# The last token tile's second layer in two column parts

## The chip, the cores and the metric

The kernel runs on one core of a Trainium2 chip. The metric is the device time of one execution in microseconds; the median of several runs is given. Beside it stands one profiled execution, whose trace lists every instruction with its engine, start and length. TensorE (PE) does the matrix products, VectorE (DVE) and ScalarE (ACT) work on tiles, GpSimd (POOL) does some copies, and SyncE (SP) issues every load and store as a DMA.

## The reference

```python
# q, k, v, alpha: (4, 8, 768, 48) float32
for t in range(S):
    state = alpha[:, :, t, :, None] * state + np.einsum('bhd,bhe->bhde', k[:, :, t], v[:, :, t])
    y[:, :, t] = np.einsum('bhd,bhde->bhe', q[:, :, t], state)
x = y.transpose(0, 2, 1, 3).reshape(3072, 384)
h = x @ w_in                  # (384, 2048)
r = np.maximum(h, 0.0)
out = (r * r) @ w_out         # (2048, 384) -> (3072, 384) float32
```

A gated linear attention over 768 steps feeds a two-layer network with a squared ReLU.

## The kernel before

The 3072 tokens are 24 tiles of 128. The attention is computed in chunks of 128 steps, 24 in all, and each chunk gives one token tile of `x`, transposed, in `xT_big`. The network runs on groups of token tiles: `GN = [4, 1, 1, 2, 2, 2, 2, 2, 2, 2, 2, 2]` (line 537), so the last group, number 11, holds tiles 22 and 23, and the one before it tiles 20 and 21.

The first layer (`add_moe1`, line 553) multiplies `w_in` with `xT_big` into a PSUM bank of 512 columns; ScalarE applies the ReLU and VectorE squares the result into `gT`. The second layer (`add_moe2`, line 592) handles one token tile: sixteen matmuls of 384 columns, one for each slice of the 2048 hidden values, add up in one PSUM bank. Each takes a 128 x 128 block of `gT` as its weights and a slice of `w_out_b` as the moving operand. One copy (`e_ev`, line 612) brings the bank into an SBUF tile `ob`, and one DMA from SP's queue (`e_out`, line 621) stores it, 128 rows of 1536 bytes.

No instruction is issued as the functions are called. Each adds an `Op` to a plan, with a duration, dependencies and a priority. `Plan.run` (line 96) takes the ops greedily in planned time: it gives each a start and an end, chooses the engine where several are allowed (ScalarE or VectorE for the copy, whichever ends first with its latency from `LAT`, line 34), and the PSUM bank, the one that is free earliest of the pool named (`takes`; for the last two groups `M2_LAST`, all five banks). Stores are planned on an engine called OUT, loads on one called DMA; both are issued on SP. A store is planned when its copy is done, and its start is then put off by `late`:

```python
            op.start = t + getattr(op, "late", 0.0)
```

For every store `late` is `OUT_LATE`, 3.5 us (line 623). At the end of `Plan.run` the whole list is sorted by start,

```python
        self.order.sort(key=lambda o: o.start)
```

and line 706 emits the instructions in this order. `pin` (line 234) keeps each engine's instructions in the order in which they are emitted, and SP's too: SP works through its queue in order, and an instruction that waits for its data holds up those behind it.

Of the kernel before, what the change touches and what calls it, by code (L numbers as in the profile page):

```python
# [8 lines left out]
FP32 = mybir.dt.float32  # L9
# [45 lines left out]
def after(op, x=0.0):  # L55
    return (op, x)
# [83 lines left out]
def kernel(  # L140
# [10 lines left out]
    nc = tc.nc  # L151
    B, H, S, D = q.shape
    HD = H * D
    P = 128
# [3 lines left out]
    d_model, d_ff = moe_w_in.shape  # L158
    n_tok = out.shape[0]
    KT = d_model // P  # L160
    FT = d_ff // P
# [6 lines left out]
    out_r = out.rearrange("(tt p) n -> tt p n", p=P)  # L168
# [7 lines left out]
    opool = ctx.enter_context(tc.tile_pool(name="opool", bufs=6))  # L176
# [15 lines left out]
        out=utri_f, in_=utri_f, compare_op=ALU.is_ge, fill=0.0,  # L192
# [10 lines left out]
    for c in range(JN):  # L203
        blk = slice(JP * c, JP * c + JP)
        nc.gpsimd.affine_select(
            out=tri4[blk, 0:JW], in_=tri4[blk, 0:JW], compare_op=ALU.is_ge, fill=0.0,
# [11 lines left out]
    w_out_b = consts.tile([P, FT, d_model], BF16)  # L218
# [15 lines left out]
    def pin(ins):  # L234
        tc.keep_in_program_order(ins)

    def mm(*a, **kw):
        pin(nc.tensor.matmul(*a, **kw))  # L238
# [4 lines left out]
    plan = Plan()  # L243
# [6 lines left out]
    M2_BANKS = sl_bank[4:1:-1]  # L250

    def psum(op, shape, dt):
        i = op.slot.bank
        return banks[i].tile(shape, dt, name=f"bank{i}")
# [6 lines left out]
    def add(eng, dur, emit, *deps, **kw):  # L261
        return plan.add(Op(eng, dur, emit, deps, **kw))
# [38 lines left out]
    def w_dep(which, f):  # L301
        return w_ready[which][[hi > f for hi in W_CUT[which][1:]].index(True)]
# [234 lines left out]
    GN = [4, 1, 1, 2, 2, 2, 2, 2, 2, 2, 2, 2]  # L537
    assert sum(GN) == NT
    GT = [sum(GN[:i]) for i in range(len(GN))]
    NG = len(GN)  # L540
    gT = {}
    NQ = 4
    NGT = 3
    FIRST = sl_bank[4:0:-1]
    M2_LAST = sl_bank[::-1]
    OUT_LATE = 3.5
    RELU_PRIO = -20.0
    RELU_PRIO0 = 0.0
    DUMMY = 1
    sq = {}  # L550
    prog = {"m1": 0.0, "m2": 0.0}

    def add_moe1(g, f0, before, lo=0, hi=None, per=1):
        hi = GN[g] if hi is None else hi
        t0, n = (GT[g] + lo) * P, (hi - lo) * P
        w = per * n
        box = {}
        op = before
        for i in range(per):
            def e_mm(i=i, f=f0 + i):  # L560
                if i == 0:
                    box["ph"] = psum(box["first"], [P, 512], FP32)
                for j in range(KT):
                    mm(box["ph"][:, i * n:(i + 1) * n], lhsT=w_in_b[:, j, f * P:(f + 1) * P],
                       rhs=xT_big[:, j, t0:t0 + n], start=(j == 0), stop=(j == KT - 1))
            deps = [C[s]["x"] for s in range(GT[g] + lo, GT[g] + hi)] + [w_dep("i", f0 + i)]
            deps += [after(op)] if op else []
            takes = M1_BANKS if i == 0 else None
            op = plan.add(Op("PE", 3 * n / 2400.0 + 0.01, e_mm, deps, takes=takes, prio=0.0, lat=0.10 if w < 512 else 0.17))
            op.moe = (1, (hi - lo) * 2.56 / FT)  # L570
            op.opens, op.closes = i == 0, i == per - 1
            if i == 0:
                box["first"] = op

        def e_relu():
            box["r"] = rpool.tile([P, 512], BF16, name="r")
            pin(nc.scalar.activation(box["r"][:, 0:w], box["ph"][:, 0:w], AF.Relu))  # L577
        rl = add("ACT", 0.055 + w / 1190.0, e_relu, op, prio=RELU_PRIO if g > 1 else RELU_PRIO0)
        box["first"].gives = rl

        def e_sq():
            if g not in gT:
                gT[g] = big.tile([P, FT, P * max(GN[g % NGT::NGT])], BF16, name=f"gT{g % NGT}", tag=f"gT{g % NGT}")
            r = box["r"][:, 0:w].rearrange("p (a n) -> p a n", a=per)
            pin(nc.vector.tensor_mul(gT[g][:, f0:f0 + per, lo * P:lo * P + n], r, r))  # L585
        fr = sq[(g - NGT, "free")] if g >= NGT else None
        o = add("DVE", 0.06 + w / 1850.0, e_sq, rl, fr, prio=SQ_PRIO)
        for i in range(per):
            sq.setdefault((g, f0 + i), []).append(o)
        return op  # L590

    def add_moe2(g, tt, before, box, quarters, pools):

        for qd in quarters:
            def e_mm(qd=qd):
                if qd == 0:
                    box["po"] = psum(box["first"], [P, 512], FP32)[:, 0:d_model]
                for kf in range(qd * FT // NQ, (qd + 1) * FT // NQ):
                    mm(box["po"], lhsT=gT[g][:, kf, tt * P:(tt + 1) * P], rhs=w_out_b[:, kf, :],
                       start=(kf == 0), stop=(kf == FT - 1))  # L600
            fs = range(qd * FT // NQ, (qd + 1) * FT // NQ) if g == 0 else range(FT)
            deps = [o for f in fs for o in sq[(g, f)]] + [w_dep("o", fs[-1] if g == 0 else FT - 1)] + ([after(before)] if before else [])
            op = plan.add(Op("PE", 0.65, e_mm, deps, takes=pools if qd == 0 else None, prio=0.1))
            op.moe = (2, 2.56 / NQ)
            if qd == 0:
                box["first"] = op
            op.lat = 0.05
            before = op
        if quarters[-1] < NQ - 1:
            return op  # L610

        def e_ev():
            box["ob"] = opool.tile([P, d_model], FP32, name="ob")
            if ev.eng == "DVE":
                pin(nc.vector.tensor_copy(box["ob"], box["po"]))
            else:
                pin(nc.scalar.copy(box["ob"], box["po"]))  # L617
        ev = add({"DVE": 0.47, "ACT": 0.38}, 0, e_ev, op, prio=-15.0)
        box["first"].gives = ev

        def e_out():
            pin(nc.sync.dma_start(out=out_r[GT[g] + tt], in_=box["ob"]))
        add("OUT", 0.55, e_out, ev, at=0.0).late = OUT_LATE
        return op
# [22 lines left out]
    for g in range(NG):  # L647
        if g == 0:
            last1 = []
            for f in range(0, FT, 4):  # L650
                for parts in FIRST_SETS:
                    for lo, hi in parts[min(f // 4, len(parts) - 1)]:
                        last1.append(add_moe1(g, f, None, lo, hi, per=4 // (hi - lo)))
                        for x in range(f + 4 // (hi - lo), f + 4, 4 // (hi - lo)):
                            last1.append(add_moe1(g, x, None, lo, hi, per=4 // (hi - lo)))
            b1 = last1[-1]
        per = 1 if g == 0 else 4 // GN[g]
        for f in range(FT if g == 0 else 0, FT, per):
            b1 = add_moe1(g, f, b1, per=per)
        if g == 0:  # L660
            boxes = [dict() for _ in range(GN[0])]
            for part in FIRST_PARTS:
                for tt in range(GN[0]):
                    b2 = add_moe2(0, tt, b2, boxes[tt], part, FIRST)
        else:
            for tt in range(GN[g]):
                b2 = add_moe2(g, tt, b2, {}, range(NQ), M2_LAST if g >= NG - 2 else M2_BANKS)
        sq[(g, "free")] = b2

    LEAD = 3.5  # L670
# [64 lines left out]
```

## Time and profile before

| | us |
|---|---|
| median of 3 runs (192.62 to 192.91) | 192.75 |
| the profiled execution | 191.59 |
| its span, first to last instruction | 189.9 |
| PE busy | 181.7 (96%) |
| DVE busy | 127.5 (67%) |
| ACT busy | 123.6 (65%) |
| second-layer matmuls, 384 of them: busy, mean of one | 71.6, 0.326 |
| copies of `ob` on ACT, 23 of 24: mean of one | 0.478 |
| stores, 24 of 192 KB: median from issue to landing | 2.7 |

A matmul's length in the trace is longer than its distance from the next, because matmuls are pipelined: to find what one more costs, the time of a run of equal ones is divided by their number. The granted clock of TensorE is 1.0 throughout. A DMA's line on SP gives the time that SP takes to issue it; the transfer comes later and is seen in the packets and in the landing.

The trace's order of loads and stores on SP ends with the last load at 122.04 us; after that SP issues nothing but stores.

### The profile page before, as it was taken

The page shows a single profiled execution, that of the slowest core. Times are in us where ns is not written, and L with a number is a line of the kernel's source. Part 1 is how long each engine was busy: PE and PEld are TensorE (multiplying, and loading weights), DVE is VectorE, ACT ScalarE, POOL GpSimd, SP SyncE. Part 2 cuts the span into 40 slices and gives each one's busy share as a digit, 9 for nine tenths or more (in the row PEclk, how much of TensorE's full clock was granted, in tenths as well). Part 3 has the DMA queues.
Part 4 walks back from the last instruction along what each step waited for, and adds up shares of the span by engine and source line. Part 5 has one row for each costly group of instructions (what it writes and reads, how often), then busy time and mean ns, then how long its engine had stood idle before and what let it go on. Part 6 is the DMA issues. An engine that isn't in the chain of part 4 may idle for free.

```text
span 189.9 us, 5238 instructions
## 1 busy us (share of the span) xinstructions
PE 181.7 (96%) x2092; PEld 137.6 (72%) x2092; DVE 127.5 (67%) x277; ACT 123.6 (65%) x285; POOL 17.5 (9%) x43
## 2 busy tenths in 40 slices
PE   7898999589999999999999999999999999999993
PEld 2577899357886788868868868868868768768661
DVE  1388889554798999858768768767857857734200
ACT  4667789155897778956955955946956746718321
POOL 8130100101111111121010010010010000000000
PEclk9999999999999999999999999999999999999999
DMA  6999996989999898999999899550110110111012
GB/s 181 226 242 264 299 342 133 350 227 196 246 234 223 183 219 188 213 175 226 202 209 232 174 239 214 108 149 0 43 45 0 47 41 5 41 41 45 12 71 83
DMA packets 104728, 30.22 MB, mean 159 GB/s; under 512 B 96256, under 2 KB 103936, under 8 KB 104704
## 3 DMA queue, kind: packets, MB, share of 16 engines
q1 hardware_dynamic: 104704, 29.89, 67.2%
q8 instruction: 16, 0.26, 0.6%
q14 instruction: 8, 0.07, 0.1%
HBM read 25.17 MB, written 4.72 MB: 157 GB/s over the span
## 4 chain that ended last, share of the span: by engine, by line
PE 84%; DMA 9%; ACT 2%; DVE 2%; issue 1%
PE bank L238 71%; DMA wo<-in_moe_w_out_dram 9%; PE bank L241 8%; PE sc L238 4%; PE st L238 2%; ACT w_out_b L294 1%; DVE w_out_b L292 1%; DVE qkT L371 0%; ACT qkT L369 0%; DVE st L492 0%; ACT A L408 0%; ACT ob L617 0%; DVE w_in_b L292 0%; DVE gT L585 0%; ACT Ainv L412 0%
## 5 line engine op out<-in xcount | busy, mean ns | idle before, releaser
L238 PE MATMUL bank<-xT_big,w_in_b 128*128 128x256 bf16 (+1 forms) x720 | 76.8, 251 | 0.0
L238 PE MATMUL bank<-w_out_b,gT 128*128 128x384 bf16 x384 | 71.6, 326 | 2.1 <-DVE w_out_b L292 2.1
L577 ACT ACTIVATE r<-bank 128x512 bf16<-128x512 f32 x96 | 56.5, 604 | 16.9 <-PE bank L238 14.9
L238 PEld LDWEIGHTS <-w_in_b 128*128 128x128 bf16 x720 | 55.4, 98 | 5.0
L238 PEld LDWEIGHTS <-gT 128*128 128x128 bf16 x400 | 35.6, 97 | 21.0 <-issue 2.1
L585 DVE TENSOR_TENSOR gT<-r 128x512 bf16<-128x512 bf16 x96 | 38.6, 428 | 14.2 <-ACT r L577 13.9
L472 DVE TENSOR_TENSOR sm<-sc,utri_b 128x512 bf16<-128x512 f32 x48 | 30.8, 683 | 3.2 <-PE sc L238 3.0
L617 ACT COPY ob<-bank 128x384 f32<-128x384 f32 x23 | 11.0, 478 | 23.7 <-PE bank L238 23.7
L431 DVE TENSOR_TENSOR qA_s<-qt,A 128x384 bf16<-128x384 f32 x24 | 13.7, 572 | 17.4 <-ACT A L408 17.4
L388 POOL CAST vb<-vt 128x384 bf16<-128x384 f32 x24 | 12.9, 538 | 122.1 <-DMA vt<-in_v_dram 64.0
L371 DVE COPY qkT<-bank 128x1024 bf16<-128x1024 bf16 (+1 forms) x23 | 15.0, 655 | 6.8 <-PE bank L241 6.8
L238 PEld LDWEIGHTS <-qkT 64*128 64x128 bf16 (+1 forms) x272 | 10.9, 95 | 6.7 <-issue 1.9
L408 ACT ACTIVATE A<-bank 128x384 bf16<-128x384 f32 x24 | 12.0, 498 | 4.9 <-PE bank L238 4.7
L497 ACT CAST sb<-st 128x384 bf16<-128x384 f32 x20 | 9.6, 478 | 7.9 <-DVE st L492 7.6
L434 DVE TENSOR_TENSOR kI_s<-kt,Ainv 128x384 bf16<-128x384 f32 x24 | 13.8, 576 | 0.0
L369 ACT CAST xn<-bank 128x384 bf16<-128x384 f32 x24 | 11.6, 483 | 1.5 <-PE bank L238 1.5
L379 ACT ACTIVATE L_s<-at 128x384 bf16<-128x384 f32 x20 | 10.5, 524 | 2.8 <-DMA at<-in_alpha_dram 2.6
L412 ACT ACTIVATE Ainv<-bank 128x384 bf16<-128x384 f32 x24 | 12.0, 502 | 0.0
L238 PE MATMUL bank<-warm 128*128 128x256 bf16 (+1 forms) x48 | 10.0, 345 | 1.3 <-DVE warm L186 1.2
L492 DVE TENSOR_TENSOR st<-st,ae_s 128x384 f32<-128x384 f32 x20 | 11.1, 556 | 0.0
L371 DVE COPY xT_big<-bank 128x384 bf16<-128x384 bf16 x23 | 8.1, 350 | 2.6 <-PE bank L241 2.5
L241 PE MATMUL bank<-ident_bf,kI_s 128*128 128x128 bf16 x96 | 9.3, 219 | 0.5 <-ACT qkT L369 0.5
(52 smaller groups left out, 138.0 us busy)
## 6 DMA issues: line engine op xcount, KB each, us to landing
qt<-in_q_dram SPq DMA_DIRECT2D x24, 192.0 KB, 3.8
kt<-in_k_dram SPq DMA_DIRECT2D x24, 192.0 KB, 3.8
vt<-in_v_dram SPq DMA_DIRECT2D x24, 192.0 KB, 3.9
out_dram<-ob SPq DMA_DIRECT2D x24, 192.0 KB, 2.7
at<-in_alpha_dram SPq DMA_DIRECT2D x20, 192.0 KB, 3.9
wo<-in_moe_w_out_dram SPq DMA_DIRECT2D x4, 768.0 KB, 9.0
wi<-in_moe_w_in_dram SPq DMA_DIRECT2D x4, 384.0 KB, 5.0
wi<-in_moe_w_in_dram SPq DMA_DIRECT2D x2, 768.0 KB, 8.3
```

Source lines behind the costliest of these rows:

```text
L238: pin(nc.tensor.matmul(*a, **kw))
L241: pin(nc.tensor.transpose(*a))
L369: pin(nc.scalar.copy(out_t, in_t))
L371: pin(nc.vector.tensor_copy(out_t, in_t))
L388: pin(nc.gpsimd.tensor_copy(d["vb"], d["vt"]))
L408: pin(nc.scalar.activation(d["A"], d["pm"][:, 0:HD].rearrange("p (h d) -> p h d", h=H), AF.Exp))
L412: pin(nc.scalar.activation(d["Ai"], d["pm"][:, 0:HD].rearrange("p (h d) -> p h d", h=H), AF.Exp, scale=-1.0))
L431: pin(nc.vector.tensor_mul(qA[:, :, 0:D], d["qt"], d["A"]))
L434: pin(nc.vector.tensor_mul(kI[:, :, 0:D], d["kt"], d["Ai"]))
L472: pin(nc.vector.tensor_mul(d["sm"][:, hh], d["sc"][:, hh], utri_b.to_broadcast([P, NP, P])))
L577: pin(nc.scalar.activation(box["r"][:, 0:w], box["ph"][:, 0:w], AF.Relu))
L585: pin(nc.vector.tensor_mul(gT[g][:, f0:f0 + per, lo * P:lo * P + n], r, r))
```

## The change

For the last tile of the last group (tile 23), `add_moe2_last` takes the place of `add_moe2`. It makes two parts, columns 0 to 256 and 256 to 384. Each part has its own PSUM bank, sixteen matmuls, a copy into its columns of one common `ob` tile, and a store of these columns. The first part's store has `late = OUT_LATE`, the second part's `late = 0.0`. All other tiles are as before.

```diff
+    LAST_CUT = 256
...
+    def add_moe2_last(g, tt, before, pools):
+        ob = {}
+        for lo, hi in ((0, LAST_CUT), (LAST_CUT, d_model)):
+            before = add_moe2_cols(g, tt, before, pools, ob, lo, hi)
+        return before
+
+    def add_moe2_cols(g, tt, before, pools, ob, lo, hi):
+        box = {}
+        w = hi - lo
+
+        def e_mm():
+            box["po"] = psum(op, [P, 512], FP32)[:, 0:w]
+            for kf in range(FT):
+                mm(box["po"], lhsT=gT[g][:, kf, tt * P:(tt + 1) * P], rhs=w_out_b[:, kf, lo:hi],
+                   start=(kf == 0), stop=(kf == FT - 1))
+        deps = [o for f in range(FT) for o in sq[(g, f)]] + [w_dep("o", FT - 1), after(before)]
+        op = plan.add(Op("PE", FT * w / 2400.0 + 0.04, e_mm, deps, takes=pools, prio=0.1, lat=0.05))
+        op.moe = (2, 2.56 * w / d_model)
+
+        def e_ev():
+            if lo == 0:
+                ob["t"] = opool.tile([P, d_model], FP32, name="ob")
+            if ev.eng == "DVE":
+                pin(nc.vector.tensor_copy(ob["t"][:, lo:hi], box["po"]))
+            else:
+                pin(nc.scalar.copy(ob["t"][:, lo:hi], box["po"]))
+        ev = op.gives = add({"DVE": 0.06 + w / 940.0, "ACT": 0.05 + w / 1190.0}, 0, e_ev, op, prio=-15.0)
+
+        def e_out():
+            pin(nc.sync.dma_start(out=out_r[GT[g] + tt][:, lo:hi], in_=ob["t"][:, lo:hi]))
+        add("OUT", 0.55 * w / d_model, e_out, ev, at=0.0).late = OUT_LATE if lo == 0 else 0.0
+        return op
...
             for tt in range(GN[g]):
-                b2 = add_moe2(g, tt, b2, {}, range(NQ), M2_LAST if g >= NG - 2 else M2_BANKS)
+                if g == NG - 1 and tt == GN[g] - 1:
+                    b2 = add_moe2_last(g, tt, b2, M2_LAST)
+                else:
+                    b2 = add_moe2(g, tt, b2, {}, range(NQ), M2_LAST if g >= NG - 2 else M2_BANKS)
```

## The prediction

> **What bounds the kernel now.** I read the page's chain first, then its end in order of time, then the timeline of the last 15 us, then the SP queue and the last store's packets.
>
> ```profile
> PE 84%; DMA 9%; ACT 2%; DVE 2%; issue 1%
> ```
>
> TensorE is the path almost throughout, but the change touches only the last token tile (tile 23), so only the end counts. The chain's last pieces (start, length, what):
>
> ```profile
> 169.86 16.79 PE bank L238 x119
> 186.65 0.02 issue
> 186.68 0.48 ACT ob L617
> ```
>
> The timeline of the end (start, length, engine, line, operation; in brackets the idle time before and what ended it):
>
> ```profile
> 176.07 10.56 PE L238 MATMUL bank<-w_out_b,gT 128*128 128x384 bf16 x64
> ...
> 179.38 8.13 SPq L622 DMA_DIRECT2D out_dram<-ob  x4
> 181.47 0.48 ACT L617 COPY ob<-bank 128x384 f32<-128x384 f32 x1 [2.12 <-PE bank L238]
> 184.07 0.48 ACT L617 COPY ob<-bank 128x384 f32<-128x384 f32 x1 [2.12 <-PE bank L238]
> 186.68 0.48 ACT L617 COPY ob<-bank 128x384 f32<-128x384 f32 x1 [2.12 <-PE bank L238]
> ```
>
> The last 64 matmuls are the second layer of tiles 20 to 23, back to back. Each tile is copied out 0.05 us after its last matmul, and its store leaves just after. Tile 22's copy ends at 184.55, so its store is long gone when tile 23's copy ends at 187.16. The last store alone, in the SP queue and in its transfers (40 slices of 187 to 190 us, 0.0725 us each):
>
> ```profile
> 187.18 0.33 SPq L622 DMA_DIRECT2D out_dram<-ob  x1
> ```
>
> ```profile
> DMA  0000000000000379999952000000000000000000
> GB/s 0 0 0 0 0 0 0 0 0 0 0 0 0 143 287 369 430 389 348 389 205 62 0 0 0 0 0 0 0 0 0 0 0 0 0 0 0 0 0 0
> ...
> out_dram<-ob SPq DMA_DIRECT2D x1, 192.0 KB, 1.8
> ```
>
> Issue at 187.18; packets from slice 13 to slice 21, that is from 187.98 to about 188.65 (0.80 us after issue, for 0.67 us); landing 1.8 us after issue, 188.98, so 0.33 us follow the packets. The span ends at 189.9, 0.92 us after the landing. The end is therefore: last matmul, copy 0.48, store 1.80, closing 0.92.
>
> **The steps. 1: matmuls.** Sixteen of 384 columns become sixteen of 256 and sixteen of 128. Pitches: (10.56 - 0.33) / 63 = 0.1624 us at 384 columns; for the others
>
> ```profile
> 170.84 5.40 PE L238 MATMUL bank<-xT_big,w_in_b 128*128 128x256 bf16 x48
> ```
>
> ```profile
> 46.55 1.33 PE L238 MATMUL bank<-xT_big,w_in_b 128*128 128x128 bf16 x21
> ```
>
> give (5.40 - 0.27) / 47 = 0.1091 and (1.33 - 0.22) / 20 = 0.0555 (0.27 and 0.22 are the mean lengths of single ones). Tile 23 starts at 176.07 + 48 x 0.1624 = 183.87. Part 1 hands over at 183.87 + 16 x 0.1091 = 185.61; part 2's last matmul starts 15 x 0.0555 later and ends 0.22 after that, at 186.66 instead of 186.63: +0.03 us. The sixteen added weight loads cost nothing: the 21 matmuls of the second row also had one load each, 98 ns by its row, and still came 55.5 ns apart. Were they not covered, 15 x (0.098 - 0.0555) = 0.64 us would come on top; the row excludes it, so that is no part of the range. The Trainium skill, "TensorE: Matmul & The Clock Gate", section "Back-to-back issue gap", gives some 81 ns for a stream of load and matmul pairs at 128 columns, and this speaks against the change: by it this term would be about 0.4 us larger. The row of 55.5 ns decides.
>
> **2: copies.** Part 1's copy (256 columns) lies under part 2's 0.84 us of matmuls, on a ScalarE that is otherwise idle; uncovered it would delay part 2's copy by its own length, below 0.48. Part 2's copy (128 columns) is in no row. Neighbours:
>
> ```profile
> L577 ACT ACTIVATE r<-bank 128x512 bf16<-128x512 f32 x48 | 28.5, 604 | 12.3 <-PE bank L238 10.9
> L617 ACT COPY ob<-bank 128x384 f32<-128x384 f32 x15 | 7.2, 478 | 19.8 <-PE bank L238 19.8
> ...
> L418 ACT ACTIVATE ae_s<-bank 64x4 f32<-64x4 f32 x9 | 1.5, 169 | 0.2
> ```
>
> Bounds are 0.17 and 0.48; the slopes between these rows (0.81 and 0.98 ns a column) put 128 columns at 0.27 and 0.23. I take 0.25. So the last copy runs from 186.71 to 186.96, 0.20 us earlier than now. If that were all, the end would come earlier.
>
> **3: stores, and the queue they pass.** Here the change moves more than it says. The instruction list is sorted by planned start, and a store's planned start is the planned end of its copy plus `late`: 3.5 for every tile, and for part 1; 0.0 for part 2. A tile's matmuls are planned at 2.6 us. Counting from the planned end of tile 22's matmuls: tile 22's store stands at 0.05 + 0.38 + 0.14 + 3.5 = 4.07; part 2's store at about 1.75 + 0.89 + 0.05 + 0.16 + 0.14 = 2.99; part 1's at 1.75 + 0.05 + 0.27 + 0.14 + 3.5 = 5.70; tile 21's at 4.07 - 2.6 = 1.47. The SP order becomes tile 21, part 2, tile 22, part 1. That SP keeps the list's order shows in mid kernel:
>
> ```profile
> 90.45 0.70 SPq L354 DMA_DIRECT2D at<-in_alpha_dram  x1
> 91.24 0.86 SPq L354 DMA_DIRECT2D qt<-in_q_dram  x1
> 92.19 2.05 SPq L622 DMA_DIRECT2D out_dram<-ob  x1
> ```
>
> That store's copy had ended at 90.12, and two loads still went ahead of it for two microseconds, as the 3.5 asks. So part 2's store, which waits for the very last copy, stands in front of tile 22's store (ready at 184.55) and part 1's (ready at about 186.2: 185.77 + 0.05 + 0.37). Nobody waits for these but the end of the kernel, which now waits for all three: 64 + 192 + 128 KB from 186.98 on, in place of 192 KB from 187.18.
>
> **4: what that queue costs.** SP's gap from the end of one issue to the next is about 0.09 us in that queue (91.24 + 0.86 to 92.19), and an issue into an empty queue 0.33, so the pitch is 0.42. Issues: part 2 at 186.98, tile 22 at 187.40, part 1 at 187.82. Packets of tile 22's store begin at 187.40 + 0.80 = 188.20. Part 1's could begin at 188.62, but share the same sixteen engines; at the rate of the present store (192 KB in 0.67) both are done at 188.20 + 0.67 x 320 / 192 = 189.32. With 0.33 the landing is 189.65, against 188.98: +0.67. Part 2's 64 KB (0.22 us of packets from 187.78) are through before and cost nothing but SP's 0.42; that pitch is the cover. The Trainium skill, "DMA: Bandwidth & Descriptors", section "Rules for kernel authors", advises to coalesce transfers, because small ones are mostly overhead; a sum by it would charge the 64 KB store its whole fixed time, which no row of this trace singles out.
>
> **Sum.** +0.03 (PE) - 0.23 (shorter copy) + 0.84 (two more issues) - 0.22 (64 KB less in the last store) + 0.25 (part 1's packets behind tile 22's) = +0.67, the same. Against the profiled execution of 191.59 (span 189.9 and 1.69 around it) that is 192.26; the median of the runs, 192.75, stands 1.16 above that execution, and carrying this over gives 193.4.
>
> Bounds. Low: a copy of 0.17 and no queueing of packets, 0.67 - 0.08 - 0.25 = +0.34. High: issues that take as long as the stores in mid kernel that found loads in flight (median of all 24 is 0.48, this row's neighbours 0.70 to 0.97): at 0.97 + 0.09 each, part 1 leaves at 189.10 and lands 0.80 + 0.45 + 0.33 later, 190.68: +1.70. I take 0.33, since the four last stores, with no loads about, all show it.
>
> **Rivals.**
> (a) The order of stores stays that of readiness. Then tile 22's and part 1's stores are gone (the latter issued at 186.2) and part 2's lands at 186.98 + 0.80 + 0.22 + 0.33 = 188.33: -0.65, a time of 192.1. This one is faster. It decides at one point: whether SP reaches tile 22's store before it meets part 2's wait. For it: the last four stores now leave 0.02 us after their own copies. Against it: the row at 92.19, and the arithmetic of 2.99 before 4.07.
> (b) The order is turned round as forecast and SP also waits for room in the queue: issues of 0.74, as the store at 86.00 us took, so a pitch of 0.83. Part 1 leaves at 188.64 and lands at 190.22: +1.24, 194.0. For it: all stores with company in the queue took 0.6 or more. Against: their company was loads of small packets.
> (c) The order is turned round, but the queue is cheap: the low bound, +0.34, 193.1, or less, within what can be told. For it: 0.20 us are gained first.
>
> **How the numbers follow.** My forecast 0.72, (a) 0.08, (b) 0.12, (c) 0.08. About 0.2% (0.39 us) can be told from no change. My forecast and (b) lie beyond it, except for a hundredth of mine: slower 0.83. (c) and that hundredth: same 0.09. (a): faster 0.08. The range leaves (a) out, takes in (c) from its end, (b), and the spread of the runs (0.15 each way): 193.0 to 194.1.
>
> **What would show it.** In the profile of the changed kernel: the stores of tiles 20 and 21 at 179.4 and 182.0, then a gap on SP until about 187, then three issues close together; no store between 182.0 and 186.9; transfers of 64, 192 and 128 KB in one block from 187.8 to 189.3; a copy of some 0.25 us ending near 186.96; sixteen matmuls of 128 columns 55 ns apart. A store issued near 184.58 would prove me wrong (rival a); issues of 0.7 us would be (b).

## The result and the profile after

The change makes the kernel slower: a median of 192.95 us against 192.16 over 22 runs each, ratio 1.0047 (95% interval 1.0024 to 1.0069), that is +0.9 us (0.5 to 1.3). The ratio is that of the means, without the one run of the kernel before that lay more than 1.5% above its fastest. The profiled execution has a span of 191.2 us.

The end in the timeline of the changed kernel (start, length, engine, line, operation; L618 and L622 are the two parts, L651 and L656 the other tiles):

```profile
184.62 0.48 ACT L651 COPY ob<-bank 128x384 f32<-128x384 f32 x1 [2.12 <-PE bank L238]
186.37 0.37 ACT L618 COPY ob<-bank 128x256 f32<-128x256 f32 x1 [1.27 <-PE bank L238]
187.26 0.27 ACT L618 COPY ob<-bank 128x128 f32<-128x128 f32 x1 [0.52 <-PE bank L238]
187.55 0.33 SPq L622 DMA_DIRECT2D out_dram<-ob  x1
187.94 0.42 SPq L656 DMA_DIRECT2D out_dram<-ob  x1
188.41 0.42 SPq L622 DMA_DIRECT2D out_dram<-ob  x1
```

Tile 22's copy ends at 185.10, part 1's at 186.74, part 2's at 187.53. All three stores leave after that, part 2's first. What SP waited for says the same: its one wait on a part's copy lasts 4.6 us, with tile 22's store ready behind it for 2.5 us.

```profile
SPq L622 <- ACT ob L618: 4.6, 1, 4.6
```

The transfers of the changed kernel, from 187.0 to 191.2 us in 40 slices of 0.105 us, and the time from issue to landing:

```profile
DMA  0000000000000495028998999960000000000000
...
out_dram<-ob SPq DMA_DIRECT2D x1, 192.0 KB, 2.0
out_dram<-ob SPq DMA_DIRECT2D x1, 128.0 KB, 1.9
out_dram<-ob SPq DMA_DIRECT2D x1, 64.0 KB, 1.5
```

First 64 KB alone, a gap, then 320 KB in one block to 189.9: tile 22's store and part 1's share the engines. The matmuls of the two parts by shape (count, busy us, mean ns):

```profile
L238 PE MATMUL bank<-w_out_b,gT 128*128 128x256 bf16 x16 | 1.9, 272 | 0.0
L238 PE MATMUL bank<-w_out_b,gT 128*128 128x128 bf16 x16 | 1.1, 219 | 0.0
```

For 128 columns, (1.1 - 0.22) / 15 = 0.06 us each; the starts in the trace lie 0.056 apart.

**How the runs were compared.** The profiled span grew by 1.3 us, more than the runs did. Tile 22's copy ends 0.55 us later than before, though the program up to there is the same. In this profile the granted clock was 0.97 over the first 60 us, where it was 1.00 before. In the eleven profiles of this study, taken on several chips, that moment lies anywhere from 182.75 to 185.25 us. Much of the difference between profiles thus arises ahead of the change, and what it is stays open. So each profile is read from the end of tile 22's copy: to the last landing, and from there to the last instruction (the closing). These repeat within 0.02 us. SP's recorded instructions include its waits.

| run | landing | closing | sum | against before | ratio of the times, 95% | SP instructions |
|---|---|---|---|---|---|---|
| before | 4.48 | 0.85 | 5.33 | | | 210 |
| the change | 5.17 | 0.98 | 6.15 | +0.82 | 1.0047 (1.0024 to 1.0069) | 210 |
| e1_ready_order | 4.00 | 1.38 | 5.38 | +0.05 | 1.0010 (0.9980 to 1.0039) | 211 |
| e2_swap_only | 5.01 | 1.02 | 6.04 | +0.71 | 1.0039 (1.0016 to 1.0062) | 209 |
| e3_tile22_first | 4.63 | 0.98 | 5.61 | +0.29 | 1.0009 (0.9983 to 1.0035) | 210 |
| e4_one_store | 4.31 | 0.85 | 5.16 | -0.17 | 0.9978 (0.9949 to 1.0006) | 210 |
| e8_both_late | 3.98 | 1.39 | 5.37 | +0.04 | 1.0007 (0.9976 to 1.0039) | 212 |
| e11_split_tile20 | 4.49 | 1.39 | 5.87 | +0.55 | 1.0056 (1.0022 to 1.0089) | 211 |
| e10_tile20_on_act | 3.98 | 0.98 | 4.97 | -0.36 | 0.9962 (0.9924 to 1.0000) | 210 |
| e12_change_again | 5.17 | 0.98 | 6.15 | +0.82 | 1.0023 (0.9989 to 1.0058) | 210 |
| e13_e10_again | 4.00 | 0.98 | 4.98 | -0.35 | 0.9989 (0.9959 to 1.0019) | 210 |

0.1% is 0.19 us. Every interval of the times takes in what the sum says. Most of them take in no change too, that of the change's own repeat (e12) among them; the times alone set three kernels apart from the one before, the change (first measurement), e2 and e11. The expectations of e1 to e4 have 5.35 and 6.10 for the sums of before and the change, and hold the closing at 0.89.

### The profile page after: what moved, and what is told of

It is laid out like the page before. It is cut to its first block, busy times and chain, and to the rows that moved or that the text cites. A ratio compares the mean times of both kernels' runs of the same rounds, so it can differ in the third digit from the quotient of the medians.

```text
span 191.2 us, 5271 instructions
## 1 busy us (share of the span) xinstructions
PE 183.1 (96%) x2108; PEld 139.6 (73%) x2108; DVE 127.9 (67%) x277; ACT 123.8 (65%) x286; POOL 18.6 (10%) x43
## 4 chain that ended last, share of the span: by engine, by line
PE 80%; DMA 11%; ACT 3%; DVE 2%; issue 1%; POOL 1%; SPq 1%; POOLq 0%; ACTq 0%
PE bank L238 68%; PE bank L241 7%; DMA vt<-in_v_dram 6%; DMA at<-in_alpha_dram 5%; PE sc L238 3%; PE st L238 1%; POOL vb L388 1%; DVE sm L472 1%; ACT A L408 1%; DVE w_out_b L292 1%; ACT gT L324 0%; ACT Ainv L412 0%; SPq L354 0%; DVE qA_s L431 0%; ACT qkT L369 0%
## 5 line engine op out<-in xcount | busy, mean ns | idle before, releaser
L238 PE MATMUL bank<-w_out_b,gT 128*128 128x384 bf16 (+2 forms) x400 | 71.6, 320 | 0.5 <-DVE w_out_b L292 0.5
L238 PEld LDWEIGHTS <-gT 128*128 128x128 bf16 x416 | 36.6, 97 | 18.7 <-issue 0.4
L388 POOL CAST vb<-vt 128x384 bf16<-128x384 f32 x24 | 14.0, 582 | 121.6 <-DMA vt<-in_v_dram 64.3
L651 ACT COPY ob<-bank 128x384 f32<-128x384 f32 x22 | 10.5, 478 | 20.5 <-PE bank L238 20.5
L238 PE MATMUL bank<-warm 128*128 128x256 bf16 (+1 forms) x48 | 10.5, 358 | 1.3 <-DVE warm L186 1.3
L241 PE MATMUL bank<-ident_bf,qA_s 128*128 128x128 bf16 x96 | 9.8, 227 | 0.2 <-DVE qA_s L431 0.2
```

The lines of the kernel that those rows point to most:

```text
L241: pin(nc.tensor.transpose(*a))
L388: pin(nc.gpsimd.tensor_copy(d["vb"], d["vt"]))
```

## The experiments

**e1: all three last stores at late 0.**

```diff
-        add("OUT", 0.55 * w / d_model, e_out, ev, at=0.0).late = OUT_LATE if lo == 0 else 0.0
+        add("OUT", 0.55 * w / d_model, e_out, ev, at=0.0).late = 0.0
...
-        add("OUT", 0.55, e_out, ev, at=0.0).late = OUT_LATE
+        add("OUT", 0.55, e_out, ev, at=0.0).late = 0.0 if g == NG - 1 else OUT_LATE
```

> The changed kernel with both parts' stores and tile 22's store at late 0, so that SP's order is tile 22, part 1 (256 columns), part 2 (128 columns). Measure: from the end of tile 22's copy to the end of the span; it is 5.35 us before and 6.10 us with the change. Theory (the turned order of stores costs, the split itself gains): part 2's store is alone at the end, issued 2.45 after tile 22's copy as with the change, packets after 0.84 for 0.34, landing 0.35 later, 0.89 to the end: 4.9 us, and a time about 0.5 us (0.25%) under the kernel before. Rival (the split itself costs, by its smaller stores, its sixteen more weight loads and one DMA more): 6.1 us as with the change, whatever the order.

Landing at 4.00, 0.48 under before: the order of stores did cost, and the split on its own gains. But the closing took 1.38, not 0.89, and ate the gain. The sum of 5.38 fits neither theory whole. The edit also put tile 22's store ahead of tile 21's; they left 0.03 and 0.41 us after tile 22's copy and ended long before the last one.

**e2: the kernel before, with only the last two stores exchanged.**

```diff
-        add("OUT", 0.55, e_out, ev, at=0.0).late = OUT_LATE
+        add("OUT", 0.55, e_out, ev, at=0.0).late = 0.0 if g == NG - 1 and tt == GN[g] - 1 else OUT_LATE
```

> The kernel before, not split, with tile 23's store at late 0, so that it stands in front of tile 22's. Same measure. Theory: tile 23's store is issued 2.63 after tile 22's copy as before, tile 22's 0.38 later, their packets take 1.25 together from 0.83 after the first issue, 0.35 to the landing, 0.89 to the end: 6.0 us, 0.6 more than before, a time 0.3% over it. Rival (the split costs): 5.35 us and no difference, since nothing is split.

No part is split, and the sum rises from 5.33 to 6.04. The two stores leave together, as the timeline and the landings of this kernel show:

```profile
186.43 0.81 SPq L622 DMA_DIRECT2D out_dram<-ob  x2
```

```profile
out_dram<-ob SPq DMA_DIRECT2D x2, 192.0 KB, 1.9
```

The turned order is enough by itself for most of what the change costs.

**e3: the changed kernel, only tile 22's store at late 0** (the second half of e1's diff).

> The changed kernel with tile 22's store alone at late 0: SP's order is tile 22, part 2, part 1. Same measure. Theory: part 2 is issued at 2.45, part 1 at 2.84, its packets from 0.85 to 0.97 after that for 0.48, landing 0.35 later, 0.89 to the end: 5.4 to 5.5 us, within 0.15 of before; of the change's 0.75 some 0.6 to 0.7 are tile 22's. Rival: 6.1 us.

Landing 4.63: taking tile 22's store out of the queue gives back 0.54, taking part 1's out as well (e1, e8) another 0.64. Both stores that were held share the cost. Of the change's 0.82, tile 22's store is thus 0.54, less than the 0.6 to 0.7 that I expected. The sum of 5.61 is 0.1 to 0.2 over my figure and 0.29 over before, where I had at most 0.15.

**e4: two parts of matmuls and copies, one store.**

```diff
-            pin(nc.sync.dma_start(out=out_r[GT[g] + tt][:, lo:hi], in_=ob["t"][:, lo:hi]))
-        add("OUT", 0.55 * w / d_model, e_out, ev, at=0.0).late = OUT_LATE if lo == 0 else 0.0
+            pin(nc.sync.dma_start(out=out_r[GT[g] + tt], in_=ob["t"]))
+        if hi == d_model:
+            add("OUT", 0.55, e_out, ev, at=0.0).late = OUT_LATE
```

> The changed kernel with both matmul parts and both copies, but one store of all 384 columns after the second copy, at late 3.5 as before: SP's order is tile 22, tile 23. Same measure. Theory: all of before's store, issued when the shorter last copy ends: 5.35 + 0.03 for the matmuls - 0.21 for the copy = 5.2 us. Rival in its form that the matmuls and copies cost: 5.4 us or more; in its form that small stores cost: 5.2 us too.

5.16: splitting matmuls and copies gains 0.17 us, as the shorter copy should. So the rival that the split itself costs, by its sixteen more weight loads or by copies, falls. That one DMA more costs is another matter: e8 and e11 below show such a cost, in the closing.

**What of the closing?** In e1, e8 and e11 SP's records at the kernel's last line hold one DRAIN of 130 ns (in e2 too, but nearer the end), which is not there before or with the change. The rows of that line for SP and for GpSimd, which SP's signal sets going (count, shortest/median/longest ns, first and last start), of before:

```profile
L730 SPq DRAIN  x3: 7/7/27, 189.1 to 189.6; - x3
L730 POOLq EVENT_SEMAPHORE  x4: 17/17/17, 189.2 to 189.8; - x4
```

of e8:

```profile
L767 SPq EVENT_SEMAPHORE  x7: 17/27/1024, 186.0 to 188.5; - x7
L767 SPq DRAIN  x3: 7/7/130, 187.6 to 188.1; - x3
L767 POOLq EVENT_SEMAPHORE  x4: 17/17/17, 187.9 to 188.4; - x4
```

Before, the other engines are set going at 189.2, 0.2 us after the landing at 189.03; in e8 at 187.9, 0.7 us after the landing at 187.14. Counting SP's records in e1 and e2, the long DRAIN is number 208 in both, and in every profile of this study number 208 starts 0.35 to 0.39 us after number 207. With 210 records that is SP's wait behind its signal; the same wait is number 207 in e2, and there it comes 0.16 us after the record before it. With 211 or 212 number 208 is the signal itself or falls just ahead of it, and all engines wait. That was the theory for the next three.

Cut at the moment when GpSimd is set going, the closing is 0.17 + 0.68 us before and in e4, 0.30 + 0.68 with the change, in e3 and e10, 0.73 + 0.66 in e1, e8 and e11, and 0.17 + 0.85 in e2. So behind the signal a late number 208 costs 0.02 us where it is a wait (210 records), while GpSimd's own records run nearly as long, and 0.19 where it is a DRAIN (209). Ahead of the signal it costs 0.4.

**e8: one word of the change undone** (part 2's store late like all others).

```diff
-        add("OUT", 0.55 * w / d_model, e_out, ev, at=0.0).late = OUT_LATE if lo == 0 else 0.0
+        add("OUT", 0.55 * w / d_model, e_out, ev, at=0.0).late = OUT_LATE
```

> The changed kernel with one word of it undone: part 2's store has late 3.5 like all others, so that SP's order is tiles 20, 21, 22, part 1, part 2. Measure: from the end of tile 22's copy to the last landing, and from there to the end of the span (the closing); before 4.48 and 0.85, with the change 5.17 and 0.98, in e1_ready_order 4.00 and 1.38. Theory (order of stores, and beside it SP's 208th recorded instruction comes 0.35 late, wherever it falls): landing 4.00 as in e1; SP has 212 recorded instructions, so the late one falls ahead of SP's signal to the other engines, closing 1.35 to 1.45; sum 5.4, time within 0.15% of before. Rival (the closing of e1 was an accident of that run): closing 0.9 to 1.0, sum 4.95, time 0.2% under before.

Landing 3.98, closing 1.39, as expected. In its queue and transfers the last store is alone:

```profile
185.61 0.33 SPq L622 DMA_DIRECT2D out_dram<-ob  x1
```

```profile
out_dram<-ob SPq DMA_DIRECT2D x1, 64.0 KB, 1.5
```

**e11: the kernel before, with tile 20's store in two parts,** eight microseconds before the end.

```diff
+        if g == NG - 2 and tt == 0:
+            add("OUT", 0.3, lambda: e_out(0, 256), ev, at=0.0).late = OUT_LATE
+            add("OUT", 0.25, lambda: e_out(256, d_model), ev, at=0.0).late = OUT_LATE
+        else:
+            add("OUT", 0.55, e_out, ev, at=0.0).late = OUT_LATE
```

> The kernel before, with tile 20's store alone issued in two parts of 256 and 128 columns, eight microseconds before the end; nothing else differs, and SP records 211 instructions in place of 210. Theory of the late 208th instruction: landing 4.48 as before, closing 1.3 to 1.4 in place of 0.85, time 0.25% over before. Rival (a closing depends on the last stores alone): landing 4.48, closing 0.85 to 0.95, no difference.

The last stores are issued as before, the landing is the same, and the closing goes from 0.85 to 1.39; the time rises by 0.56% (0.22 to 0.89). Of the 0.54, the late instruction is 0.42. Another 0.13 is that one store more moves the last store to another semaphore, the third of the five that SP waits for at the end, where it was the fifth. The expectation had not seen this second part. The long DRAIN is there again:

```profile
L734 SPq DRAIN  x3: 7/7/130, 187.5 to 188.3; - x3
```

**e10: e8, with tile 20's store issued by ScalarE.**

```diff
-            pin(nc.sync.dma_start(out=out_r[GT[g] + tt], in_=box["ob"]))
+            q = nc.scalar if g == NG - 2 and tt == 0 else nc.sync
+            pin(q.dma_start(out=out_r[GT[g] + tt], in_=box["ob"]))
```

> e8_both_late with tile 20's store issued from ScalarE's queue, which takes two instructions from SP: 210 recorded, as before. Theory: landing 4.00, closing 0.98 as with the change (the last store's semaphore is again not the last one that SP waits for), sum 4.98, 0.35 us (0.2%) under before; faster than both kernels. Rival (accident): the same closing as e8_both_late, whichever that is.

SP is back at 210 records, the closing at 0.98, the sum 0.36 us under before, and the DRAIN is short:

```profile
L768 SPq DRAIN  x3: 7/7/8, 188.1 to 188.6; - x3
```

**e12 and e13: the change and e10 once more, side by side.**

> The changed kernel once more, beside e13 on one chip, since the differences are small against the spread of the runs. From the end of tile 22's copy: landing 5.17, closing 0.98, sum 6.15 (0.8 over before) if the profile's end explains the whole difference; time 0.3 to 0.6% over before.

> e10_tile20_on_act once more, beside the changed kernel. Landing 3.99, closing 0.98, sum 4.97: 1.2 us (0.6%) under e12 and 0.36 us (0.2%) under before. If its time is not under that of before, the gain read from the profile's end is lost elsewhere.

The ends repeat to 0.02 us. The change's time is 0.23% over before here, with an interval from -0.11 to 0.58%: the repeat fits the first measurement, but would not show a slower kernel by itself. The medians on that chip are 191.79 and 190.65 us: e10 is 1.1 us under the change (0.8 by the means). Against before it is -0.38% and -0.11% in its two measurements, with intervals that reach 1.0000 and 1.0019. The profile says 0.18%; the times alone don't tell it from no change. So against the changed kernel the times of twelve runs each and the profile's end point the same way (0.8 to 1.1 and 1.2 us); against the one before, the gain rests on the profile alone.

## Why the prediction was right, point by point

- **The time.** Forecast was +0.67 us, measured +0.9 (0.5 to 1.3) by the runs and +0.82 by the profile's end. As a time, 193.4 was forecast and 193.0 to 194.1 given as the range; the median of 192.95 lies 0.05 below its lower end, because the three runs that I counted from (192.75) stood 0.6 us above the median of all 22.
- **Matmuls, +0.03.** Measured +0.04 from tile 22's copy to the last matmul's end (2.09 to 2.12). The pitch of 55.5 ns held with all sixteen weight loads beside it. The figure of some 81 ns that the Trainium skill gives in "TensorE: Matmul & The Clock Gate", section "Back-to-back issue gap", would have made it 0.4 us more, by an estimate of mine; the measured pitch decides.
- **The last copy, 0.25.** It took 0.266, and part 1's 0.372 lay under the matmuls as assumed.
- **The order of stores.** As read from the sort: tile 21 at 182.53, then nothing until part 2 at 187.55, tile 22, part 1. e2 shows the turned order at work without the split.
- **The queue, two pitches of 0.42.** Measured 0.38 and 0.47, together 0.86 for 0.84. The second and third issue took 0.42 where I had 0.33, and the gaps 0.05 where I had 0.09. That the last issue began within 0.02 us of the forecast is luck in part: the longer second issue and the shorter gaps nearly cancel. Rival (b), issues of 0.74, did not happen.
- **The packets.** Landing moved by +0.69, from 4.48 to 5.17, where the sum had +0.67. Tile 22's packets began 0.92 us after its issue, where I had 0.80, and the 320 KB took 1.05 us, where I had 1.12: two errors of opposite sign again. That all three transfers would make one block, as I wrote among the signs, did not come true and did not follow from my own times either.
- **The closing, held at 0.92.** Here a term was missing. It was 0.85 before and 0.98 after, +0.13: the semaphore of the last store is the third of five that SP goes through at the end, and no longer the last, so that two more follow it. With that the end is +0.82 where +0.67 was forecast. That it stayed at 0.13 is luck: the change adds a store to SP's queue, but tile 22's store and part 1's, held behind part 2's, have no record of a wait ahead of them, so SP has 210 records as before. With the order kept (e8) it has 212, and the closing is 1.39.
- **Rival (a), the order kept: -0.65, a time of 192.1.** The point on which it turned was named rightly, but its price was wrong. e8 is that case: the landing came 0.49 earlier, not 0.65 (the 64 KB took 1.53 us from issue to landing, where I had 1.35), and the closing 0.53 later, which I hadn't thought of. Had the order been kept, the kernel would have been as fast as before, not faster. A third of the bytes took 1.53 us, where 192 KB took 1.85. The Trainium skill, "DMA: Bandwidth & Descriptors", section "Rules for kernel authors", says that transfers under 64 KB are mostly overhead and advises to coalesce. That reason fits these numbers, though this store is just 64 KB. The advice does not fit the landing here: one store (e4) landed at 4.31, two in the order kept (e8) at 3.98; only the closing turns that round (sums 5.16 and 5.37).

## What to carry to other kernels

Where a planner sorts a list by planned start, read where a new entry lands among its neighbours before costing the entry: one store with its own lateness held two others, and that cost more than the split gained. When a gain of some 0.2 us at the end is at stake, read the end in two pieces, to the last landing and from there on, because here one more instruction on SP moved the second by half a microsecond (0.85 to 1.39 in e11). And where runs spread by a per cent, compare such pieces in the profiles beside the times.

## What was not expected

The closing depends on how many instructions SP has had: 0.85 to 0.98 us with 210 records and 1.38 to 1.39 with 211 or 212, whether the added ones stand at the end (e8) or one stands eight microseconds earlier (e11); with 209 (e2) it was 1.02. In all profiles the 208th record starts 0.35 to 0.39 us after the one before. That it is tied to the place in SP's program is shown; what SP does in that time is not, since no record of SP covers it.

The trace of transfers holds one thing that goes with it. In each of the eleven profiles a single packet of 8 KB, of the kind that the trace calls instruction, starts 0.62 to 0.65 us after the 208th record, wherever that record falls, and its queue (q14) had none for 31 us before. It is the last digit 1 in the rows of before and of e8 (185 to 192 us, 40 slices of 0.175 us):

```profile
DMA  0049940000000000069930000000010000000000
...
q14 instruction: 1, 0.01, 0.4%
```

```profile
DMA  0001991056000000001000000000000000000000
...
q14 instruction: 1, 0.01, 0.3%
```

This fits a fetch of instructions set off at that place. But the packet comes after the late record, so it can't be what that record waited for. The Trainium skill, "Runtime: NRT & Kernel Launch", section "Instruction fetch mechanics", says that instructions are refilled in blocks and that crossing a block is mostly hidden; the packets are a hint of such a crossing, but no run here shows that it is the cause, and if it is, it was not hidden.
